# A fixed TensorE round for an attention and gated feed-forward kernel, with another start and paced loads

## The chip, the cores and the metric

The kernel runs on one core of one Trainium2 chip. The metric is the device time of one execution in microseconds (us).

## The reference, cut to what matters

```python
# q, k, v: (4 batches, 8 heads, 768 positions, 64); blocks of 32 positions
scores = q @ k.T / 8
mask   = |block_i - block_j| <= 1, or first/last block row or column, or one of 3 sampled blocks per row
attn   = softmax(where(mask, scores, -1e9)) @ v
x      = attn as (3072 tokens, 512)
out    = (sigmoid(x @ w_gate) * (x @ w_val)) @ w_out        # 512 -> 1536 -> 512, float32 out
```

## The kernel before

All matrices are float16, sums float32. Work is cut into 12 groups of 256 queries (4 batches times 3), and each group into 4 head pairs, so there are 48 head pairs. A head pair needs:

- three **score tiles** (128 keys x 2, 2 heads, 256 queries). The head dimension is 64, so a score matmul fills half of the array's rows, and the two heads run side by side. A tile takes two banks of PSUM.
- an exponential of each tile on ScalarE (ACT), and a multiplication by the mask on VectorE (DVE).
- **values**: 24 full-array matmuls, one bank.

A group of 256 queries then needs 12 **gate** steps (8 matmuls of 256 columns, one bank, a tanh on ACT, a product on DVE) and two **outputs** of 12 matmuls of 512 columns, one bank each.

The program is not written in the order in which it runs. Every operation goes into a plan with an estimated time, what it reads and writes, and a priority; a greedy list scheduler in Python fixes the order on each engine before anything is built. Each engine then runs its list strictly in order and waits where a real duration differs from the plan.

```python
SINGLE, PAIR = (7, 6, 5, 4), (0, 2)          # banks of all else; pairs of banks of the scores
...
st = psb([2, 512], homes=(0, 2, 4) if n < 1 else PAIR, span=2)      # a score tile
o  = P.op("PE", 0.43 if masked else 0.215, scores, ..., prio=seq, mode="row", behind=scored[-1:])
o.paired = not masked                         # after full-array work, wait until two tiles fit
...
if e == "PE":
    if o.mode != mode:                        # the plan's price of going from "row" to "full" or back
        dur += 0.095
```

The start: the mask tables go out on ACT's DMA queue, the identity and the first keys on SyncE's (SP), everything else on GpSimd's (POOL). TensorE (PE) is kept busy with dummy matmuls ("spins" on a tile of zeros) until data are there:

```python
P.op("SP", 0.4, lambda: nc.sync.dma_start(ident16(), id_h.ap()), writes=[ident16], prio=-99, dma=0.1)
P.op("ACT", 0.4, lambda: nc.scalar.dma_start(sbi(), sampled_blocks), writes=[sbi], prio=-90, dma=0.1)
P.op("ACT", 0.4, lambda: nc.scalar.dma_start(mi(), mi_h.ap()), writes=[mi], prio=-89, dma=0.1)
...
o = self.spin_op(0.11 if now < 12.0 else 0.06, fresh)     # a dummy matmul, where PE has nothing planned
```

The softmax here doesn't subtract the row's maximum and nothing guards it: scores larger than these inputs give would overflow.

Of the kernel before, what the change touches and what calls it, by code (L numbers as in the profile page):

```python
# [20 lines left out]
NCH = 3  # L21
# [8 lines left out]
NMASK = 1  # L30
EDGES = [0, 768, 1536]
FIRST = [
    ("q", 0), ("k", 1), ("q", 1), ("k", 2), ("q", 2), ("v", 0), ("k", 3), ("q", 3), ("v", 1), ("v", 2), ("v", 3),
# [22 lines left out]
class Op:  # L56
    def __init__(self, ways, deps, allocs, prio, mode, dma, behind):
        self.ways, self.deps, self.allocs = ways, deps, allocs
        self.prio, self.mode, self.dma, self.behind = prio, mode, dma, list(behind)
        self.eng = self.start = self.end = self.seen = None  # L60
        self.paired = False
        self.slack = 0.0
# [5 lines left out]
class Plan:  # L68
# [16 lines left out]
    def op(self, eng, dur, fn, reads=(), writes=(), after=(), prio=0, mode=None, dma=0.0, behind=(), alt=()):  # L85
        deps, allocs = list(after), []
        ways = {eng: (dur, fn), **{e: (t, f) for e, t, f in alt}}
        o = Op(ways, deps, allocs, prio, mode, dma, behind)
        for b in reads:
            deps.extend(b.writers)  # L90
            b.users.append(o)
        for b in writes:
            if not b.users and b.ring is not None:
                allocs.append(b)
                if b.ring in self.queued:
                    b.turn = self.queued[b.ring]
                    self.queued[b.ring] += 1
            else:
                deps.extend(b.users if b.ring is None else b.writers)
            b.users.append(o)  # L100
            b.writers.append(o)
        self.ops.append(o)
        return o

    def run(self):
# [23 lines left out]
        def places(allocs, eng):  # L129

            t, where, taken = 0.0, [], set()
            for b in allocs:
                if b.ring in self.queued:
                    s = slot(b.ring, 0, eng) if b.turn == at[b.ring] else None
                    where.append(at[b.ring] % len(self.rings[b.ring]))
                else:
                    can = []
                    for i in b.homes:
                        at_, old = now, self.rings["ps"][i : i + b.span]
                        for k, u in enumerate(old):  # L140
                            s = None if i + k in taken else clear(u, eng)
                            at_ = None if s is None or at_ is None else max(at_, s)
                        if at_ is not None:
                            can.append((at_, self.spun is not None and self.spun in old, len(can), i))
                    s, _, _, i = min(can) if can else (None, 0, 0, None)
                    taken.update(range(i, i + b.span) if can else ())
                    where.append(i)
                if s is None:
                    return None, None
                t = max(t, s)  # L150
            return t, where
# [11 lines left out]
        while left:  # L163
            wake = []
            for e in LAT:
# [54 lines left out]
                if o.dma:  # L220
                    first = now + (3.2 if e == "POOL" else 1.9)
                    if o.dma > 0.15:
                        first = dma_free = max(dma_free, first) + o.dma
                    o.seen = first + 0.3 + o.slack
                else:
                    o.seen = o.end + LAT[e]
# [27 lines left out]
def kernel(  # L254
# [15 lines left out]
    e24_np = np.zeros((128, NJ * 128), np.float16)  # L270
    for r in (0, 64):
        e24_np[r : r + NB] = tok.reshape(1, -1) // BLK == np.arange(NB)[:, None]
# [34 lines left out]
    SINGLE, PAIR = (7, 6, 5, 4), (0, 2)  # L307
# [16 lines left out]
    def one(shape, dt, name):  # L324
# [11 lines left out]
    P.op("SP", 0.4, lambda: nc.sync.dma_start(ident16(), id_h.ap()), writes=[ident16], prio=-99, dma=0.1)  # L336
    P.op("ACT", 0.4, lambda: nc.scalar.dma_start(sbi(), sampled_blocks), writes=[sbi], prio=-90, dma=0.1)
    P.op("ACT", 0.4, lambda: nc.scalar.dma_start(mi(), mi_h.ap()), writes=[mi], prio=-89, dma=0.1)
    P.op(
        "SP", 0.5, lambda: nc.sync.dma_start(e24().rearrange("b j q -> b (j q)"), e24_h.ap()),  # L340
        writes=[e24], prio=-94.5, dma=0.5,
    )
# [19 lines left out]

    stage, half16, tr, v16 = {}, {}, {}, {}
# [41 lines left out]
    def load_half(nm, b, p, prio, dur=0.72):  # L405
        c = sb(f"{nm}16" if nm != "v" else "vh", [128, 2, NJ, 64], f16)
        half16[nm, b, p] = stage[nm, b, p] = c
        o = P.op(
            "POOL", dur, lambda: nc.gpsimd.dma_start(c(), src[nm][b][:, 2 * p : 2 * p + 2]),  # L409
            writes=[c], prio=prio, dma=1.0,  # L410
        )
        o.slack = 0.3 + b
        return o

    def turn_pe(nm, b, p, js, prio, behind=()):

        n = js.stop - js.start
        c = half16[nm, b, p]
        if (nm, b, p) not in tr:
            tr[nm, b, p] = sb(f"{nm}T", [128, NJ, 128], f16)  # L420
        t = tr[nm, b, p]
        g = psb([n, 128], f16)

        def go():
            for j in range(n):
                for hd in range(2):
                    nc.tensor.transpose(
                        g()[hd * 64 : hd * 64 + 64, j, :], c()[:, hd, js.start + j], ident16()
                    )

        P.op("PE", 0.06 * n, go, reads=[c, ident16], writes=[g], prio=prio, mode="col", behind=behind)
        P.op(
            "DVE", 0.1 + 0.075 * n, lambda: nc.vector.tensor_copy(t()[:, js], g()), reads=[g], writes=[t],
            prio=prio,
        )
# [11 lines left out]
    every, early, later = slice(0, NJ), slice(0, 2), slice(2, NJ)  # L447
    load("k", 0, 0, -95)
    t, c = stage["k", 0, 0], one([128, 2, NJ, 64], f16, "k16_first")
    half16["k", 0, 0] = c  # L450
    P.op("ACT", 0.83, lambda t=t, c=c: nc.scalar.copy(c(), t()), reads=[t], writes=[c], prio=-67)
    for i, (nm, p) in enumerate(FIRST):
        last_in = load_half(nm, 0, p, -60 + i, 0.82 if i == 0 else 0.72)
    for p in range(NP):
        turn_pe("k", 0, p, every, -40 + 2 * p)
        turn_pe("q", 0, p, early, -39.5 + 2 * p)
        cast_v(0, p, -30 + p)
# [21 lines left out]
    def load_out(s, prio, behind):  # L479
        def go():  # L480
            ins = nc.gpsimd.dma_start(wo()[:, 4 * s : 4 * s + 4], wov[:, 4 * s : 4 * s + 4])  # L481
            if s == 2:
                landed["o"] = ins

        o = P.op(
            "POOL", 0.8, go,
            prio=prio, dma=2.65, behind=behind,
        )
        for f in range(4 * s, 4 * s + 4):
            w_out[f] = o  # L490
# [16 lines left out]
    def blocks():  # L507
# [7 lines left out]
        for r in (0, 64):  # L515
            d.tensor_tensor(mb16()[:, r : r + NB], eqs()[:, 0], eqs()[:, 1], op=ALU.max)

    P.op("DVE", 0.65, blocks, reads=[sbi, mi], writes=[mb16, eqs], prio=-70)
    for c, j0, n in ((0, 0, 2), (1, 2, 4)):
# [6 lines left out]
            reads=[mb16, e24], writes=[pb], prio=-69 + 32.5 * c, mode="full",  # L526
# [6 lines left out]
            reads=[pb], writes=[bias], prio=-69 + 32.5 * c,  # L533
        )

    mask_ops = {}
# [31 lines left out]
    def attend(n, p, seq):  # L568
# [3 lines left out]
        for tt in range(NCH):  # L572
            st, pt = psb([2, 512], homes=(0, 2, 4) if n < 1 else PAIR, span=2), sb("pt", [128, 2, 2, CH], f16)
# [19 lines left out]
            )  # L593
            scored.append(o)
            o.paired, o.twin = not masked, psb([2, 512], homes=PAIR, span=2)
# [32 lines left out]
        valued[n, p] = P.op("PE", 0.79, values, reads=[*pts, v16[b, p]], writes=[o], prio=seq + 0.1, mode="full")  # L628
# [42 lines left out]
    def ffn(g, seq):  # L671
# [4 lines left out]
        for f in range(NF):  # L676
            both = psb([512], homes=range(7, -1, -1) if last else SINGLE)
# [36 lines left out]
        for tt in range(w // 128):  # L714
# [5 lines left out]
            for u in range(parts):  # L720
                m = slice(u * wd, u * wd + wd)
                py = psb([DM], homes=range(7, -1, -1) if g >= len(GROUPS) - 2 else SINGLE)
                for f0 in range(0, NF, 4):

                    def go(f0=f0, tt=tt, py=py, m=m):
                        for f in range(f0, f0 + 4):
# [7 lines left out]
                            "PE", 0.862 / parts, go, reads=[hts[g, f] for f in range(f0 + 4)], writes=[py],  # L734
# [18 lines left out]
    seq, turned = 0, []  # L753
    for n in range(B * NCH):
        b, c = divmod(n, NCH)
        if n == 1:
            for p in range(NP):
                turn_pe("q", 0, p, later, 9.0, [valued[0, 1]])
            build_mask(1, 11.5, scored[:1])
# [5 lines left out]
        if b + 1 < B:  # L765
            for p in range(NP) if c == 0 else ():
# [5 lines left out]
                for nm in "kqv":  # L772
                    o = load(
                        nm, b + 1, p, seq + p, behind=turned[:-2][-2:],
                        **(dict(after=[w_out[8]], sync="o") if b == 0 else {}),
                    )
                    o.slack = 1.5
                for nm in "kq":
# [4 lines left out]
    for (n, p), o in valued.items():  # L783
        g = group_of[n][0] - 2
        if g >= 0:
            o.behind.append(gates[2 * NF * (g + 1) - 1])
    P.run()
# [30 lines left out]
```

## Time and profile before

297.87 us (median of 3; 297.75 to 298.46). The lines of the page that say what the kernel spends: span, busy time by engine, PE's busy tenths in 40 slices, and the granted clock of PE in tenths.

```profile
span 295.6 us, 8119 instructions
...
PE 289.7 (98%) x3417; PEld 211.3 (72%) x3417; DVE 192.4 (65%) x448; ACT 212.5 (72%) x329; POOL 13.4 (5%) x22
...
PE   8999998999999999999999999999999999999995
...
PEclk9999999999999999999999999999999999999999
```

PE is the bound. "Busy" is not the same as useful, though. The timeline of PE in the steady part shows what is lost (columns: start, duration of the group, engine, line, operation, matrices, shapes, count; in later views [idle time before, and what ended it, the "releaser"]; L582 scores, L683 gates, L727 outputs, L621 values):

```profile
190.77 0.61 PE L582 MATMUL psum<-qT,kT 64*128 64x256 f16 x8
191.32 2.76 PE L727 MATMUL psum<-wo,h 128*128 128x512 f16 x12
194.01 0.61 PE L582 MATMUL psum<-qT,kT 64*128 64x256 f16 x8
194.56 0.61 PE L683 MATMUL psum<-x,wg 128*128 128x256 f16 x4
195.00 0.60 PE L683 MATMUL psum<-x,wv 128*128 128x256 f16 x4
```

Take starts, not ends, since matmuls overlap. Gates to gates is 0.44 us for four matmuls. Two score tiles are four side-by-side pairs of 0.109 us, which is 0.436, but the next group starts 0.55 us after them (194.01 to 194.56); and the outputs need 12 x 0.2158 = 2.59 us, but 2.69 pass until the next scores. So each batch of score tiles costs about 0.10 us going in and 0.11 coming out, 0.21 us in all. PE never stands idle there for any releaser; the time goes at the change of the array's layout. The Trainium skill ("TensorEngine Tiling (Array Packing)", section "Key Properties") says that a change of tiling mode drains TensorE, that is, lets the work in it run out; it names no cost. The trace fits that: the first gate's weight load starts at 194.55, with its matmul, where later ones start 0.1 us ahead of theirs.

In the trace of before there are 77 batches of scores, 49 of them from the 17th head pair on (46 of two tiles, 3 of one). The count ahead of the 17th, 28, leaves out short pieces between mask steps and looks past transposes and dummies; with every uninterrupted run of score matmuls counted it is 42.

### The profile page before, as it was taken

What the parts mean: (1) busy time and instruction counts of PE and PEld (TensorE: products, weight loads), DVE (VectorE), ACT (ScalarE), POOL (GpSimd) and SP (SyncE); (2) the same over time, 40 slices, a digit from 0 to 9 for tenths busy, and PEclk for the clock granted to TensorE, in tenths of its full rate; (3) what the DMA queues carried; (4) which work ended last, traced back from release to release, by engine and by line L of the source; (5) the groups of instructions that cost most, each with busy time, mean ns of one, the idle gap of its engine ahead of it and who ended that gap; (6) DMA issues with size and microseconds to landing.
All of it is one profiled execution on the core that took longest, in us unless ns stands there. A gap on an engine that the chain in (4) does not pass through costs nothing.

```text
span 295.6 us, 8119 instructions
## 1 busy us (share of the span) xinstructions
PE 289.7 (98%) x3417; PEld 211.3 (72%) x3417; DVE 192.4 (65%) x448; ACT 212.5 (72%) x329; POOL 13.4 (5%) x22
## 2 busy tenths in 40 slices
PE   8999998999999999999999999999999999999995
PEld 7676875786587587578578678667767768778673
DVE  3659995799677677577767657657657656634230
ACT  2699987889888789797588578478478478434331
POOL 8630000000000000000000000000000000000000
PEclk9999999999999999999999999999999999999999
DMA  7999969999999969940210210210120120120102
GB/s 157 199 211 210 206 171 283 311 297 271 272 244 248 228 96 308 172 115 2 62 47 0 65 47 3 55 54 2 31 77 2 27 83 3 27 82 0 38 35 72
DMA packets 50316, 35.56 MB, mean 120 GB/s; under 512 B 31080, under 2 KB 47336, under 8 KB 50280
## 3 DMA queue, kind: packets, MB, share of 16 engines
q1 hardware_dynamic: 43520, 28.16, 38.5%
q0 software_dynamic: 6688, 6.88, 14.1%
q8 instruction: 26, 0.43, 0.6%
q14 instruction: 10, 0.08, 0.1%
q10 hardware_dynamic: 72, 0.01, 0.0%
HBM read 28.55 MB, written 6.29 MB: 118 GB/s over the span
## 4 chain that ended last, share of the span: by engine, by line
PE 82%; DMA 13%; POOL 2%; issue 1%; SPq 0%; ACT 0%; DVE 0%; POOLq 0%
PE psum L683 40%; PE psum L727 21%; PE psum L582 10%; PE psum L621 10%; DMA wo<-in_moe_w_out_dram 8%; DMA q<-in_q_dram 3%; DMA vs<-in_v_dram 2%; POOL q L409 1%; POOL k L409 1%; POOL wo L481 1%; SPq L371 0%; POOL vh L409 0%; PE psum L657 0%; DVE h L709 0%; ACT tg L702 0%
## 5 line engine op out<-in xcount | busy, mean ns | idle before, releaser
L598 ACT ACTIVATE pt<-psum 128x1024 f16<-128x1024 f32 x144 | 143.9, 1025 | 38.1 <-PE psum L582 37.9
L606 DVE TENSOR_TENSOR pt<-pt,mask 128x1024 f16<-128x1024 f16 x132 | 90.4, 689 | 44.1 <-ACT pt L598 43.7
L683 PE MATMUL psum<-x,wg 128*128 128x256 f16 x576 | 86.6, 273 | 0.2 <-DVE h L709 0.2
L683 PE MATMUL psum<-x,wv 128*128 128x256 f16 x576 | 86.7, 273 | 0.0
L709 DVE SCALAR_TENSOR_TENSOR h<-tg,psum 128x256 f16<-128x256 f32 x144 | 56.8, 416 | 21.3 <-ACT tg L702 21.2
L727 PE MATMUL psum<-wo,h 128*128 128x512 f16 (+1 forms) x300 | 66.8, 371 | 0.0
L702 ACT ACTIVATE tg<-psum 128x256 f32<-128x256 f32 x144 | 55.2, 388 | 14.1 <-PE psum L683 11.3
L683 PEld LDWEIGHTS <-wg 128*128 128x128 f16 x576 | 54.7, 98 | 11.5 <-issue 4.2
L683 PEld LDWEIGHTS <-wv 128*128 128x128 f16 x576 | 53.8, 98 | 11.9 <-issue 6.1
L727 PEld LDWEIGHTS <-h 128*128 128x128 f16 x300 | 27.5, 98 | 30.6 <-issue 4.0
L582 PE MATMUL psum<-qT,kT 64*128 64x256 f16 x576 | 48.5, 272 | 0.3 <-ACT pt L598 0.3
L621 PEld LDWEIGHTS <-pt 128*128 128x128 f16 x1152 | 40.4, 97 | 4.3 <-issue 1.3
L621 PE MATMUL psum<-v,pt 128*128 128x65 f16 x1152 | 42.2, 193 | 0.0
L582 PEld LDWEIGHTS <-kT 64*128 64x128 f16 x576 | 23.4, 94 | 14.5 <-issue 11.0
L744 ACT ACTIVATE y<-psum 128x512 f32<-128x512 f32 (+1 forms) x21 | 12.1, 577 | 21.9 <-PE psum L727 20.0
L632 DVE TENSOR_TENSOR x<-psum,rz 128x256 f16<-128x256 f32 x48 | 20.4, 424 | 1.6
L629 DVE RECIPROCAL rz<-psum 128x4 f32<-128x4 f32 x48 | 8.6, 179 | 15.6 <-PE psum L621 15.1
L356 PE MATMUL psum<-zero 128*128 128x128 f16 x49 | 5.7, 296 | 1.0 <-DVE zero L335 1.0
L582 PE MATMUL psum<-bias,e 64*128 64x256 f16 x48 | 6.3, 273 | 0.0
L402 ACT CAST q<-qs 128x768 f16<-128x768 f32 x6 | 5.0, 833 | 1.8 <-DMA qs<-in_q_dram 1.8
L552 DVE TENSOR_SCALAR mask<-psum 128x512 f16<-128x512 f32 x9 | 6.1, 683 | 0.0
L356 PEld LDWEIGHTS <-zero 128*128 128x128 f16 x49 | 4.7, 138 | 1.8 <-DVE zero L335 1.0
(43 smaller groups left out, 72.4 us busy)
## 6 DMA issues: line engine op xcount, KB each, us to landing
out_dram<-y SPq DMA_DIRECT2D x23, 256.0 KB, 2.4
ks<-in_k_dram SPq DMA_DIRECT2D x13, 384.0 KB, 4.1
qs<-in_q_dram SPq DMA_DIRECT2D x12, 384.0 KB, 5.4
vs<-in_v_dram SPq DMA_DIRECT2D x12, 384.0 KB, 5.0
wg<-in_moe_w_gate_dram POOLq DMA_DIRECT2D x2, 768.0 KB, 14.2
wv<-in_moe_w_val_dram POOLq DMA_DIRECT2D x2, 768.0 KB, 17.0
wo<-in_moe_w_out_dram POOLq DMA_DIRECT2D x3, 512.0 KB, 21.8
q<-in_q_dram POOLq DMA_DIRECT2D x4, 192.0 KB, 6.2
```

Source lines behind the costliest of these rows:

```text
L356: "PE", dur, lambda: nc.tensor.matmul(t(), zero(), zero(), start=True, stop=True),
L582: nc.tensor.matmul(st()[:, hd, jj * CH : (jj + 1) * CH], l[r, 2 * tt + jj, :], m[r, 2 * c : 2 * c + 2, :], start=not (own and masked), sto ...
L598: lambda st=st, pt=pt: nc.scalar.activation(pt().rearrange("p h j q -> p h (j q)"), st(), AF.Exp, scale=SCALE),
L606: nc.vector.tensor_tensor(t, t, mask()[:, c, tt].unsqueeze(1).to_broadcast([128, 2, 512]), op=ALU.mult)
L621: nc.tensor.matmul(o()[:, 2 * jq + hd, 0:65], pts[j // 2]()[:, hd, j % 2, jq * 128 : jq * 128 + 128], v_[:, hd, j, 0:65], start=(j == 0), ...
L629: P.op("DVE", 0.2, lambda: nc.vector.reciprocal(rz(), o()[:, :, 64:65]), reads=[o], writes=[rz], prio=seq - 5)
L632: lambda: nc.vector.tensor_tensor(x16().rearrange("p j (h d) -> p (j h) d", d=64), o()[:, :, 0:64], rz().to_broadcast([128, 4, 64]), op=AL ...
L683: nc.tensor.matmul(t()[:, z : z + w], wt()[:, i, f * 128 : (f + 1) * 128], xT[g, i]()[:, 0:w], start=(i == 0), stop=(i == NP - 1),)
L702: lambda tg=tg, a=pair[0]: nc.scalar.activation(tg()[:, 0:w], a[0]()[:, a[1] : a[1] + w], AF.Tanh, scale=0.5),
L709: lambda tg=tg, a=pair[1], h_=h_: nc.vector.scalar_tensor_tensor(h_()[:, 0:w], tg()[:, 0:w], 1.0, a[0]()[:, a[1] : a[1] + w], op0=ALU.add, ...
L727: nc.tensor.matmul(py()[:, m], hts[g, f]()[:, tt * 128 : (tt + 1) * 128], wo()[:, f, m], start=(f == 0), stop=(f == NF - 1),)
L744: lambda py=py, y=y, m=m: nc.scalar.activation(y()[:, m], py()[:, m], AF.Copy, scale=0.5),
```

## The change

Its intent: from the 17th head pair on, PE repeats one round for each head pair: three score tiles together (six of the eight banks), one output slice, the values of the head pair before, three gate steps, two output slices. Banks are no longer parted: all work may use all eight. The loads of a later batch wait for a given round. And the start is rebuilt, to bring the first score earlier. The core of the diff (cut):

```diff
+FETCH = ((7, 1), (1, 2))
+CHAIN, GLAG, OLAG, ROUND = 16, 5, 9, "SoVgggoo"
+LAND_K, LAND_Q, E24 = 4.0, 4.7, 4.2        # when the plan takes the first loads to be there
-    SINGLE, PAIR = (7, 6, 5, 4), (0, 2)
+    SINGLE, PAIR = range(7, -1, -1), (0, 2, 4, 6)
-    P.op("SP", 0.4, lambda: nc.sync.dma_start(ident16(), id_h.ap()), writes=[ident16], prio=-99, dma=0.1)
-    P.op("ACT", 0.4, lambda: nc.scalar.dma_start(sbi(), sampled_blocks), writes=[sbi], prio=-90, dma=0.1)
-    P.op("ACT", 0.4, lambda: nc.scalar.dma_start(mi(), mi_h.ap()), writes=[mi], prio=-89, dma=0.1)
+    P.op("ACT", 0.4, lambda: nc.scalar.dma_start(ident16(), id_h.ap()), writes=[ident16], prio=-99, dma=0.1, lands=3.0)
+    P.op("ACT", 0.6, lambda: nc.scalar.dma_start(sbi(), sampled_blocks), writes=[sbi], prio=-98, dma=0.1, lands=3.4)
+    P.op("ACT", 0.4, lambda: nc.scalar.dma_start(mi(), mi_h.ap()), writes=[mi], prio=-97, dma=0.1, lands=3.8)
...  (the first keys in one float32 load, cast in two parts; a third of the first queries in a load of its own;
...   the mask for the first 256 queries built first, the rest later; output steps of two matmuls, not four)
-            o.paired, o.twin = not masked, psb([2, 512], homes=PAIR, span=2)
+            o.paired, o.twin = not masked and 4 * n + p < CHAIN, psb([2, 512], homes=PAIR, span=2)
+    chain, gi, oi = [], 6 * (CHAIN - GLAG), 3 * max(0, CHAIN - OLAG)
+    for m in range(CHAIN, len(score) + 8):
+        for step in ROUND:
+            if step == "S":
+                chain += score[m] if m < len(score) else []
+            elif step == "V":
+                chain += value[m - 1 : m]
+            elif step == "g":
+                chain += gates[gi : gi + 2]
+                gi += 2
+            elif m >= OLAG:
+                chain += outs[oi : oi + 1]
+                oi += 1
+    chain += outs[oi:]
+    for a, z in zip(chain, chain[1:]):
+        z.behind.append(a)                    # in the plan, each only after the one ahead of it
+    for m, o in late_loads:
+        o.behind.append(score[m][-1])         # loads paced by round
```

## The prediction

> **What bounds the kernel now.** TensorE. The page gives PE 289.7 us busy of 295.6 (98%), ACT 72%, DVE 65%; the clock is 1.0 throughout. The view of waits puts only about 3 us on PE; the chain of waits is 82% PE. Busy is not work, so I added start-to-start intervals of the trace: a gate matmul of 256 columns 109.2 ns, an output matmul of 512 columns 215.8, a value matmul 31.8, a pair of half-array score matmuls 109. (The Trainium skill, "TensorE: Matmul & The Clock Gate", section "Back-to-back issue gap", gives N/2.4 + 2.5 ns; the trace agrees.) From the first score (8.38 us) to the last matmul (292 us) there are 283.6 us, of which 262.9 are such work. Of the other 20.7 about 15 are switches between half-array scores and full-array work: the timeline shows 0.095 us lost going in and as much coming out, 0.19 us for a batch of scores, and there are 77 batches. Real waits after 8.4 us are about 2.5 us (0.9 of it at 48 us).
>
> **What the change does.**
> 1. Fixed round from the 17th head pair on: three score tiles together. The 96 tiles there now go in 49 or 50 batches; after, 32. That saves 17 to 18 switches of 0.19 us: 3.4 us, all on the critical path, as PE never waits there. The matmul work is unchanged: a round is 0.65 + 0.19 scores, 1.30 output, 0.76 values, 2.62 gates: 5.5 us.
> 2. Will the round stall? It costs ACT 3 exponentials (0.97), 3 tanh (0.38), half an eviction (0.3): 4.3 us; DVE 3 masks (0.65), 3 products (0.42), 0.6: 3.8 us. Six banks for scores leave two, for an output in progress and the last gate; that gate's bank comes free about 0.3 us into the round, a finished output's at about 1.0 us, before values at 1.28. Narrow but enough; I allow 0.8 us of new waits.
> 3. The start: the first head pair's keys and half its queries come by themselves, cast in parts. The first score should start near 6.2 us (estimate: landing, plus 0.35 cast, 0.3 transposes, 0.3 copy). But up to 25 us PE has only scores and values, and ACT (9 tenths busy there, 1.0 us a tile) feeds those, so not all is kept: 1.5 us.
> 4. Loads paced by round, all eight banks for all: no work saved; the wait at 48 us may go: 0.4 us. The tail (3.2 us after the last matmul) stays.
>
> Sum: -3.4 - 1.5 - 0.4 + 0.8 = -4.5 to -5: **predicted 293.0 us, 8 in 10 between 289.8 and 295.8**. Faster by over 2% (under 291.9): 0.33; within 2%: 0.65; slower by over 2%: 0.02.
>
> **What would show it.** Score batches from the 17th head pair: 32, of 12 matmuls each; from that pair's first score to the last matmul 3 to 4 us shorter. PE waits inside rounds under 1 us in total; round period near 5.5 us. First score near 6.2 us, but the first gate hardly earlier than 25.35. ACT and DVE busy times equal within 3 us.
>
> **What would make it wrong.** Real exponentials and masks take longer than the plan's (0.915, 0.61 us), so a round could wait for banks; 0.2 us in each of 32 rounds takes all back. Transposes of attention outputs share the DMA queue with paced loads; a late one stalls gates that can no longer be reordered. Or the weights land earlier and PE gains more at the start: under 291 us.

## The result, and the profile after

294.38 us (median of 4; 293.13 to 295.25), before 297.81 (median of 4). The ratio is 0.988, with a 95% interval of 0.984 to 0.992. (Here and below a ratio is the mean time of one kernel's fast runs over that of the other's in the same rounds, so it is not quite the ratio of the medians.) The page after:

```profile
span 292.5 us, 8112 instructions
...
PE 285.4 (98%) x3411; PEld 212.2 (73%) x3411; DVE 193.4 (66%) x451; ACT 210.2 (72%) x329; POOL 13.4 (5%) x22
...
PE   5999999999999999999999999999999999999995
...
PEclk9799999999999999999999999999999999999999
```

Two digits have changed for the worse, at the very start: PE's first slice and the clock's second one. The rest is PE at 9. One round in the steady part (L617 scores, L764 outputs, L658 values, L720 gates):

```profile
191.75 0.83 PE L617 MATMUL psum<-qT,kT 64*128 64x256 f16 x12
192.51 0.61 PE L764 MATMUL psum<-wo,h 128*128 128x512 f16 x2
192.95 0.93 PE L658 MATMUL psum<-v,pt 128*128 128x65 f16 x24
193.71 0.60 PE L720 MATMUL psum<-x,wg 128*128 128x256 f16 x4
...
196.33 1.03 PE L764 MATMUL psum<-wo,h 128*128 128x512 f16 x4
197.29 0.83 PE L617 MATMUL psum<-qT,kT 64*128 64x256 f16 x12
```

Every round from the 18th head pair on takes 5.54 or 5.55 us from score to score, to the last scores; no round waits. There are 33 batches of scores from the 17th head pair on, 31 of them of 12 matmuls (three tiles), where before had 49. In front of the 17th there are 19, where before had 28 (31 and 42 with every uninterrupted run counted).

Now the start. The timeline after, cut to what the first score waits for (ACTq and SPq lines are DMA issues):

```profile
0.73 0.41 ACTq L342 DMA_DIRECT2D ident<-bb_ident  x1
...
1.91 0.30 ACTq L344 DMA_DIRECT2D mi<-bb_mdet_iota  x1
...
6.74 0.22 DVE L540 TENSOR_TENSOR eqs<-mi,sbi 24x72 f32<-24x72 f32 x1 [5.08 <-DMA mi<-bb_mdet_iota]
...
7.55 0.28 PE L557 MATMUL psum<-e,mb 24*128 24x256 f16 x1 [2.36 <-DVE mb L546]
7.69 0.41 ACT L475 CAST q_a<-q_in 128x256 f16<-128x256 f32 x1 [2.69 <-DMA q_in<-in_q_dram]
...
8.91 0.85 PE L441 MATMUL psum<-ident,k 128*64 128x128 f16 x12
9.16 0.37 ACT L449 COPY qT<-psum 128x256 f16<-128x256 f16 x1 [0.69 <-PE psum L441]
...
10.48 0.40 PE L617 MATMUL psum<-bias,e 64*128 64x256 f16 x2
...
10.66 0.42 PE L617 MATMUL psum<-qT,kT 64*128 64x256 f16 x2
...
10.88 0.42 PE L617 MATMUL psum<-bias,e 64*128 64x256 f16 x2
```

The same places before:

```profile
1.38 0.31 ACTq L338 DMA_DIRECT2D mi<-bb_mdet_iota  x1
...
3.78 0.22 DVE L509 TENSOR_TENSOR eqs<-mi,sbi 24x72 f32<-24x72 f32 x1 [2.52 <-DMA mi<-bb_mdet_iota]
...
8.38 0.28 PE L582 MATMUL psum<-bias,e 64*128 64x256 f16 x2
...
8.50 0.27 PE L582 MATMUL psum<-qT,kT 64*128 64x256 f16 x2
...
8.61 0.27 PE L582 MATMUL psum<-bias,e 64*128 64x256 f16 x2
```

A table `mi` of 4.5 KB landed at 6.7 us instead of 3.8, although it was issued only 0.5 us later. In the trace's DMA records its data packets ran between 4.4 and 6.1 us, after the identity (1.8 to 3.2) and the sampled blocks (3.3 to 4.2) on the same queue and between packets of the key load and of POOL's loads; the engines were 90% busy or more from 2.7 us on. Before, they ran between 2.6 and 3.3 us, though the engines were as busy from 2.7 us on there too. The Trainium skill ("DMA: Bandwidth & Descriptors", section "Queues, rings and completion order") says that each DMA engine goes round the queues packet by packet; these records agree with that. The query slice landed 5.9 us after its issue, at 7.7, where the plan had 4.7. And the first score stood about 1 us more behind the transposes of the second head pair (from 8.91), which the plan had put ahead of it: its own queries were in place at 9.53.

So the first score came at 10.48 us, 2.1 us later than before, not 2.2 us earlier. This is one execution. Four of the experiments below keep these first instructions as they are, but for a dummy, and their profiles have the table in use at 5.6 (no_pace), 5.7 (four_banks), 5.8 (no_round) and 6.9 us (split_scores), and the first score at 8.3, 8.4, 9.7 and 10.8 us. So the start of the changed kernel varies by more than 2 us from one execution to the next, and a first score that comes 1 us earlier in one profile doesn't show by itself what an edit did. And the score pairs started 0.21 us apart, not 0.11 (10.66 to 10.88 against 8.50 to 8.61): PE ran at half clock. The trace's clock records have full clock from 4.92 to 8.34 us, half to 11.75, then full; in the window before, PE had stood idle for 2.4 us, since the planned dummies ran out at 5.2. The skill ("TensorE: Matmul & The Clock Gate", "What's actually happening") describes this: a window of 3413 ns whose activity sets the clock, full or half. Here too the change came in steps of 3.41 us.

To add up the two profiled executions, I took from elapsed time what PE's work needs at full rate (0.1092 us for a gate matmul, 0.2158 for an output of 512 columns, 0.0318 for values, 0.1092 for a score pair, 0.03 and 0.06 for transposes, dummies nothing). What is left is lost time, in us:

| stretch | before | after | difference |
|---|---|---|---|
| to the first score (8.38 / 10.48 us) | 7.1 | 9.3 | +2.2 |
| from there to the 17th head pair (78.9 / 82.9 us) | 10.2 | 8.5 | -1.7 |
| from there to the last matmul (292.1 / 289.2 us) | 10.5 | 7.1 | -3.4 |

The sum, -2.9 us, is the difference of the last matmuls' starts (292.11 and 289.17).

Of the -1.7 us in the second row, waits that went away make up most. Before, PE waited 1.4 us there, the longest time at 49 us for an attention output that it had to transpose (from the view of waits):

```profile
PE psum L657 <- DVE x L632: 0.7, 1, 0.7
```

After, it waited 0.1 us in the whole stretch. Against that, half clock until 11.75 us cost after about 0.6 us (half of 1.27).

### The profile page after: what moved, and what is told of

It is laid out like the page before. It is cut to its first block, busy times and chain, and to the rows that moved or that the text cites. A ratio compares the mean times of both kernels' runs of the same rounds, so it can differ in the third digit from the quotient of the medians.

```text
span 292.5 us, 8112 instructions
## 1 busy us (share of the span) xinstructions
PE 285.4 (98%) x3411; PEld 212.2 (73%) x3411; DVE 193.4 (66%) x451; ACT 210.2 (72%) x329; POOL 13.4 (5%) x22
## 4 chain that ended last, share of the span: by engine, by line
PE 91%; ACT 4%; DMA 2%; DVE 1%; issue 1%; ACTq 0%; DVEq 0%
PE psum L720 43%; PE psum L764 22%; PE psum L617 12%; PE psum L658 12%; ACT pt L635 3%; DMA mi<-bb_mdet_iota 2%; PE psum L441 1%; PE psum L579 1%; DVE pt L643 1%; PE psum L694 0%; PE psum L364 0%; ACT y L781 0%; ACTq L343 0%; PE psum L557 0%; DVE k L409 0%
## 5 line engine op out<-in xcount | busy, mean ns | idle before, releaser
L635 ACT ACTIVATE pt<-psum 128x1024 f16<-128x1024 f32 x144 | 139.0, 1031 | 21.4 <-PE psum L617 21.1
L720 PE MATMUL psum<-x,wv 128*128 128x256 f16 x576 | 86.5, 273 | 0.0
L720 PE MATMUL psum<-x,wg 128*128 128x256 f16 x576 | 86.4, 272 | 0.0
L764 PE MATMUL psum<-wo,h 128*128 128x512 f16 (+1 forms) x300 | 76.0, 372 | 0.1
L720 PEld LDWEIGHTS <-wv 128*128 128x128 f16 x576 | 55.7, 98 | 7.6 <-issue 1.3
L720 PEld LDWEIGHTS <-wg 128*128 128x128 f16 x576 | 53.3, 98 | 8.3 <-issue 1.5
L658 PEld LDWEIGHTS <-pt 128*128 128x128 f16 x1152 | 42.6, 98 | 9.6 <-issue 0.6
L617 PE MATMUL psum<-qT,kT 64*128 64x256 f16 x576 | 45.2, 272 | 0.0
L658 PE MATMUL psum<-v,pt 128*128 128x65 f16 x1152 | 44.3, 193 | 0.0
L764 PEld LDWEIGHTS <-h 128*128 128x128 f16 x300 | 25.9, 98 | 22.4 <-issue 8.0
L617 PEld LDWEIGHTS <-kT 64*128 64x128 f16 x576 | 25.1, 94 | 19.1 <-issue 16.1
L781 ACT ACTIVATE y<-psum 128x512 f32<-128x512 f32 (+1 forms) x23 | 13.3, 580 | 12.7 <-PE psum L764 12.7
L617 PE MATMUL psum<-bias,e 64*128 64x256 f16 x48 | 6.3, 289 | 0.0
L402 ACT CAST v<-vs 128x768 f16<-128x768 f32 x7 | 5.9, 842 | 0.0
L409 DVE CAST q<-qs 128x768 f16<-128x768 f32 x10 | 5.5, 553 | 0.5 <-DMA qs<-in_q_dram 0.5
```

The costliest lines, as they stand in the source:

```text
L617: nc.tensor.matmul(st()[:, hd, jj * CH : (jj + 1) * CH], l[r, 2 * tt + jj, :], m[r, 2 * c : 2 * c + 2, :], start=not (own and masked), sto ...
L635: lambda st=st, pt=pt: nc.scalar.activation(pt().rearrange("p h j q -> p h (j q)"), st(), AF.Exp, scale=SCALE),
L658: nc.tensor.matmul(o()[:, 2 * jq + hd, 0:65], pts[j // 2]()[:, hd, j % 2, jq * 128 : jq * 128 + 128], v_[:, hd, j, 0:65], start=(j == 0), ...
L720: nc.tensor.matmul(t()[:, z : z + w], wt()[:, i, f * 128 : (f + 1) * 128], xT[g, i]()[:, 0:w], start=(i == 0), stop=(i == NP - 1),)
L764: nc.tensor.matmul(py()[:, m], hts[g, f]()[:, tt * 128 : (tt + 1) * 128], wo()[:, f, m], start=(f == 0), stop=(f == NF - 1),)
L781: lambda py=py, y=y, m=m: nc.scalar.activation(y()[:, m], py()[:, m], AF.Copy, scale=0.5),
```

## The experiments

Theory A: the round gains by saving switches of the array's layout; the new start loses about 2 us. Rival B: the start is hidden behind ACT and the loads and worth nothing either way, so that the whole gain is the 17 switches that the prediction counted. Theory D was added later: the start's loss is partly PE's clock.

The numbers of all runs, each beside the runs of before on the same chip:

| run | median (lowest to highest) us | ratio to before | 95% interval |
|---|---|---|---|
| after | 294.38 (293.13 to 295.25) | 0.988 | 0.984 to 0.992 |
| round_old_start | 292.85 (291.75 to 294.66) | 0.984 | 0.979 to 0.989 |
| start_old_round | 299.62 (299.27 to 300.34) | 1.006 | 1.004 to 1.009 |
| mask_first | 293.41 (292.5 to 294.13) | 0.984 | 0.981 to 0.988 |
| split_scores | 307.67 (306.66 to 308.64) | 1.033 | 1.029 to 1.037 |
| start_fixed | 295.26 (294.38 to 296.2) | 0.993 | 0.989 to 0.997 |
| no_round | 297.03 (295.97 to 297.8) | 0.999 | 0.995 to 1.002 |
| no_pace | 298.2 (297.05 to 300.2) | 1.003 | 0.998 to 1.009 |
| four_banks | 331.82 (one run) | | |
| more_spins | 293.31 (292.17 to 293.48) | 0.985 | 0.982 to 0.987 |
| mask_first_spins | 293.44 (292.71 to 293.98) | 0.986 | 0.984 to 0.988 |
| best | 292.53 (291.79 to 292.83) | 0.983 | 0.980 to 0.985 |
| eight_banks | 299.43 (298.54 to 300.46) | 1.006 | 1.003 to 1.008 |

All gave correct results. In the sections below, "late" batches are those from the 17th head pair on.

### The two halves of the change alone

round_old_start is the changed kernel with the first 8 us of before:

```diff
 # on the changed kernel: back to before's identity, tables and mask building
-    P.op("ACT", 0.4, lambda: nc.scalar.dma_start(ident16(), id_h.ap()), ..., lands=3.0)
+    P.op("SP", 0.4, lambda: nc.sync.dma_start(ident16(), id_h.ap()), ..., dma=0.1)
...
-    P.op("SP", 0.5, lambda: nc.sync.dma_start(k_in(), src["k"][0][:, 0:2]), ...)     # and q_in, their casts
+    load("k", 0, 0, -95)
...
```

> The changed kernel with the first 8 us of the kernel before (its loads, queues, casts and mask building), all else as changed. Theory A (the round and the free bank order save about 25 switches of 0.19 us, 4.8 us; the new start loses about 2 us because the first score comes at 10.5 instead of 8.4 us): first score near 8.4 us, 292.0 to 292.8 us. Rival B (the start is hidden behind ScalarE and the weights and is worth nothing either way; the whole 3.4 us is the 17 switches): 294.2 to 294.6 us.

start_old_round is the kernel before with just those lines of the new start.

> The kernel before with only the new start. Theory A: first score near 10.5 us and 299.3 to 300.3 us, slower than before by about 2 us. Rival B: 297.6 to 298.0 us.

The new start alone made the old kernel slower by 0.6%, its interval clear of 1. The time is as A expected, and it is against B. The way there is not quite A's: in the profile the first score came at 9.54 us, not 10.5, and 0.6 us of the loss is a longer wait at 52.6 us (1.36 us, where before waited 0.74 at 49 us), since the scheduler makes the whole plan anew when the start changes. The round with the old start gave 292.85, just above what A expected (292.0 to 292.8); its interval overlaps that of the changed kernel, so time alone doesn't show that it is faster. Its runs fell apart: 291.75, 292.08, 293.61 and 294.66 (of which 290.0, 290.3, 290.7 and 292.9 lie between the first instruction and the last). The last is the profiled one; in it PE stood idle for 1.0 us ahead of the first query transposes (not at all in the profile of before), had half clock from 7.2 to 14.0 us, and the first score came at 9.1 us.

### What the mask tables' place in the queue is worth

```diff
 # on the changed kernel: the tables ahead of the identity on ACT's queue
-    ... writes=[ident16], prio=-99, dma=0.1, lands=3.0)
-    ... writes=[sbi], prio=-98, dma=0.1, lands=3.4)
-    ... writes=[mi], prio=-97, dma=0.1, lands=3.8)
+    ... writes=[ident16], prio=-96.5, dma=0.1, lands=3.8)         # a higher number goes later
+    ... writes=[sbi], prio=-98, dma=0.1, lands=3.0)
+    ... writes=[mi], prio=-97, dma=0.1, lands=3.4)
```

> The changed kernel with the two small mask tables ahead of the identity matrix on their DMA queue. Theory A (TensorE sat idle 2.4 us for the table that landed at 6.7 us behind 32 KB of identity, then ran at half clock): the table lands before 4.5 us, no wait of over 1 us on it, first score near 9.5 us (then the query slice, which landed at 7.7 us, is last), 292.5 to 293.6 us. Rival B: 294.2 to 294.6 us. Rival C (the table is late because all 16 DMA engines are full, whatever its place in the queue): it still lands after 6 us and nothing changes.

The timeline of this run, at the same places as before:

```profile
1.41 0.30 ACTq L344 DMA_DIRECT2D mi<-bb_mdet_iota  x1
...
4.72 0.22 DVE L540 TENSOR_TENSOR eqs<-mi,sbi 24x72 f32<-24x72 f32 x1 [3.06 <-DMA mi<-bb_mdet_iota]
...
9.35 0.40 PE L617 MATMUL psum<-bias,e 64*128 64x256 f16 x2
```

The table landed 2.0 us earlier (0.8 us or more before that of any execution with the old order) and the first score came 1.1 us earlier, with the query slice now last (7.0 us); the median fell by 1.0 us, though the intervals overlap. The rival that its place in the queue does not matter is out. The clock was no better here: half until 12.9 us in the profiled run, and that took the 1.1 us back (half of the 2.25 us for which the scores ran longer at half clock): the last matmul started at 289.0 us, against 289.2. So the traces don't show where the 1.0 us of the medians came from.

### What a switch costs

```diff
 # on the changed kernel
-CHAIN, GLAG, OLAG, ROUND = 16, 5, 9, "SoVgggoo"
+CHAIN, GLAG, OLAG, ROUND = 16, 5, 9, "sosVsgggoo"        # s: one score tile
```

> The changed kernel with the three score tiles of a round apart, each between full-array work: 96 batches for the same 96 tiles instead of 32 or 33. If a switch into and out of half-array scores costs 0.19 us, 63 more cost 12 us: 306 to 307 us, round period 5.92 us instead of 5.545. If instead the gain came from the order of the other work or from the banks, the time stays within 2 us of 294.4.

The timeline of PE in one round of this run:

```profile
200.41 0.39 PE L617 MATMUL psum<-qT,kT 64*128 64x256 f16 x4
200.74 0.60 PE L764 MATMUL psum<-wo,h 128*128 128x512 f16 x2
201.28 0.39 PE L617 MATMUL psum<-qT,kT 64*128 64x256 f16 x4
201.60 0.94 PE L658 MATMUL psum<-v,pt 128*128 128x65 f16 x24
```

95 late batches instead of 33, and 13.3 us more in the medians: 0.21 us for each. The round's period is 5.97 us instead of 5.545, which is the same 0.21 us twice. The order of the other work is as it was and no round waits, so the number of batches is what counts. Expected were 306 to 307 us; most of the excess is the switch being 0.21 rather than 0.19 (62 times 0.02 is 1.2 us).

### The round without its parts

no_round leaves the plan free to the end, with all else of the change:

```diff
-CHAIN, GLAG, OLAG, ROUND = 16, 5, 9, "SoVgggoo"
+CHAIN, GLAG, OLAG, ROUND = 99, 5, 9, "SoVgggoo"
```

> The changed kernel without its fixed round (the plan orders TensorE freely to the end), all else kept. If the round's gain is the 16 to 17 switches it saves from the 17th head pair on: 49 or more batches there, 297.3 to 298.0 us. If the eight banks for all alone gave the gain: within 0.7 us of 294.4.

297.03 us, a little under the range, and no longer different from before. With four pairs of banks to choose from the free plan makes 45 late batches, fewer than the 49 I had expected. The lost time from the 17th head pair on is 10.2 us against 7.1 with the round; the 12 batches explain 2.3 to 2.5 of the 3.1.

four_banks keeps the round but parts the banks as before:

```diff
-    SINGLE, PAIR = range(7, -1, -1), (0, 2, 4, 6)
+    SINGLE, PAIR = (7, 6, 5, 4), (0, 2)
```

> The changed kernel with the banks parted as before: scores in two pairs of banks, all else in the other four. The third score tile of a round must then wait for the first one's exponential (about 1.0 us and 0.4 us of latencies, against 0.22 us for the second tile): round period 6.5 to 6.9 us instead of 5.545, 325 to 335 us in all. If six banks are not what makes the round work: within 2 us of 294.4.

```profile
200.41 0.61 PE L617 MATMUL psum<-qT,kT 64*128 64x256 f16 x8
202.08 0.39 PE L617 MATMUL psum<-qT,kT 64*128 64x256 f16 x4 [1.06 <-ACT pt L635]
```

The third tile stands 1.06 us before the first one's exponential has freed its banks; the round's period is 6.6 to 6.8 us, and the kernel takes 331.82 us. So three tiles together need six banks, and six banks need the freed partition.

eight_banks is the other way about: before, with only the freed banks.

```diff
 # on the kernel before, with the new way to choose a bank
-    SINGLE, PAIR = (7, 6, 5, 4), (0, 2)
+    SINGLE, PAIR = range(7, -1, -1), (0, 2, 4, 6)
...
-            st, pt = psb([2, 512], homes=(0, 2, 4) if n < 1 else PAIR, span=2), ...
+            st, pt = psb([2, 512], homes=PAIR, span=2), ...
```

> The kernel before with only the freed banks (any work in any of the eight banks, scores in any of four pairs); no round, no new start, no pacing. The plan then makes 66 batches of scores instead of 77. If fewer batches are what the banks give: 11 times 0.19 us, 295.4 to 296.2 us, useful work and waits unchanged, and fewer batches ahead of the 17th head pair too (the 1.7 us there that the prediction had not foreseen). If the banks alone give nothing and the gain there came from elsewhere: 297.3 to 298 us.

This was a clear miss. The trace has some 61 batches, 16 fewer than before (41 of them late, by any way of counting), and yet the kernel is 0.6% slower. Lost time was 10.9 us from the first score to the 17th head pair (before 10.2) and 11.7 after it (before 10.5). The waits of PE in this run:

```profile
...
PE psum L659 <- DVE x L634: 0.7, 1, 0.7
PE psum L546 <- ACT pt L600: 0.5, 1, 0.5
PE psum L584 <- ACT pt L600: 0.5, 1, 0.5
```

Scores and mask steps (L584, L546) wait for exponentials to give banks back, and there are repeated stops of 0.2 us at gates after 180 us, each ending just as a product on DVE ends. So where all work shares the banks, a free order saves switches and pays for them with waits. Only the round, which was laid out so that nothing waits for a bank, keeps the saving. That the small stops are bank waits follows from their timing alone; the view names no releaser for them.

### Pacing of the loads

```diff
 # on the changed kernel
-    for m, o in late_loads:
-        o.behind.append(score[m][-1])
```

> The changed kernel with loads of later batches not paced by the round. If pacing saves no work and only avoids waits of the attention transposes behind loads: 0 to 1 us slower, waits of TensorE on transposed inputs after 90 us if anything; theory: 294.2 to 295 us.

A second miss, and a larger one: 298.2 us, all of the gain gone. From the waits of PE:

```profile
PE psum L720 <- DMA x<-x: 2.2, 1, 2.2
...
PE psum L720 <- DVE x L669: 0.8, 1, 0.8
```

From 94.1 to 96.2 us the gates wait 2.2 us for the transpose of an attention output, which goes over the same DMA queue as the unpaced loads; this is one of the risks that the prediction had named. In a fixed round nothing else may go ahead. This idle time also cost clock: the records have half clock from 97.2 to 100.7 us. From the 17th head pair on (84.1 us here) the lost time is 13.1 us, against 7.1 in the changed kernel; the two waits above and the half clock make up 4.7 of these 6 us (3.0 waited, and half of 3.4); four shorter waits at 84 to 86 and at 130 us, 1.5 us together, are about the rest. The first score came at 8.3 us here, so the loss would have been larger with the start of the changed kernel's profile.

### The start repaired by order of loads

```diff
 # on mask_first: query slice and keys ahead of the mask pattern on SP's queue,
 # landing times as traces showed them, the first head pair's scores planned first
-LAND_K, LAND_Q, E24 = 4.0, 4.7, 4.2
+LAND_K, LAND_Q, E24 = 4.7, 3.4, 5.0
...
-                writes=[st], prio=seq, mode="row", behind=scored[-1:],
+                writes=[st], prio=seq if n or p else -50, mode="row", behind=scored[-1:],
...
-        o.slack = 0.3 + b
+        o.slack = 1.8
```

> The changed kernel with the mask tables first on their queue, the query slice and the keys first on the other, landing times in the plan set to what the traces showed, and the first head pair's scores planned ahead of the second pair's transposes. Theory A (each us by which the first score comes earlier is worth about 1 us until some 7 us, because TensorE is the bound from there on): first score at 6.6 to 7.6 us, 290.0 to 292.0 us. Rival B (before 25 us ScalarE and the weights bound it, so a start earlier than that of the kernel before, 8.4 us, is worth nothing more): 292 to 293 us, with TensorE waiting between 10 and 27 us.

It failed, and does not decide between A and B. The table and the query slice were there by 3.5 us, but now the identity, last on its queue, came at 6.7:

```profile
6.73 0.30 PE L441 MATMUL psum<-ident,q_a 128*64 128x128 f16 x4 [1.70 <-DMA ident<-bb_ident]
```

The first score came at 8.49 us, at half clock until 11.3 us; and the plan, which follows from every number in it, brought new waits: 1.5 us of PE between 73 and 89 us. The small transfer issued last was late in both: the table after, the identity here.

### The clock

```diff
 # on the changed kernel: more dummy matmuls in the same idle stretches of the plan
-                        o = self.spin_op(0.11 if now < 12.0 else 0.06, fresh)
+                        o = self.spin_op(0.06 if now < 12.0 else 0.06, fresh)
```

> The changed kernel with 29 more dummy matmuls in the first idle stretch (64 instead of 35) and 5 more by the first score, nothing else. Theory D (TensorE's idle time before 8 us puts its clock to half at 8 to 12 us, just when real work begins, and that, with the late first score, is what the new start loses): no half clock after 8.5 us, transposes and first scores at full rate, 292.2 to 293.6 us, and the runs closer together than the 2.1 us of the changed kernel. Rival: half clock there costs nothing since the stretch to 25 us is bound by ScalarE and loads: 294 to 294.8 us.

The timeline of PE in this run:

```profile
1.40 6.18 PE L364 MATMUL psum<-zero 128*128 128x128 f16 x64 [1.40 <-DVE zero L340]
7.50 0.28 PE L557 MATMUL psum<-e,mb 24*128 24x256 f16 x1
...
9.58 0.28 PE L617 MATMUL psum<-bias,e 64*128 64x256 f16 x2
9.70 0.27 PE L617 MATMUL psum<-qT,kT 64*128 64x256 f16 x2
9.80 0.27 PE L617 MATMUL psum<-bias,e 64*128 64x256 f16 x2
```

The mask work starts when it did (7.50 against 7.55): the table was late again (in use at 6.3 us), and the longer row of dummies held PE 0.4 us beyond the mask that was made from it (ready at 7.1). But full clock holds from 6.5 us on, the pairs start 0.11 us apart, and the first score comes 0.9 us earlier. The last matmul starts at 288.4 us instead of 289.2. The median is 293.31, 1.1 us under the changed kernel (0.9 by the ratios) and in the range of D; the runs span 1.3 us instead of 2.1. The two ratios' intervals overlap between 0.984 and 0.987, so the time alone would not prove it. What the trace shows is full clock at the first scores, in the one execution that was profiled; an earlier first score is within what the start varies by, and no_pace had full clock there (until 97 us) without more dummies.

mask_first_spins adds the tables' order of mask_first:

> The same dummy matmuls with the mask tables first on their queue. Theory D: first score near 8.8 us at full clock, 291.4 to 292.6 us. Rival: as the run with the mask tables first alone, 293.0 to 293.8 us.

293.44: no better than the dummies alone, and a miss for D. The reason that its trace shows: 59 dummies, most of them at half clock, held PE until 7.5 us, so that the mask work started no earlier than in more_spins though the mask was ready at 5.5. Dummies that outlast the wait become the wait.

### A version that beats both

best takes the round, banks and pacing of the changed kernel, the loads of before, and the mask of the first 256 queries built first, then:

```diff
-                writes=[st], prio=seq, mode="row", behind=scored[-1:],
+                writes=[st], prio=seq if n or p else -38.75, mode="row", behind=scored[-1:],
...
-                        o = self.spin_op(0.11 if now < 12.0 else 0.06, fresh)
+                        o = self.spin_op(0.08 if now < 12.0 else 0.06, fresh)
```

> A try at a version better than both: round, banks and pacing of the changed kernel, the loads of the kernel before, mask building for the first query chunk alone, first scores planned before the second pair's transposes, dummy matmuls planned at 0.08 us. First score near 7.8 to 8.2 us at full clock: 290.3 to 291.8 us. If what the plan does later (waits at 60 to 100 us, as in an earlier attempt) eats it: 292 to 294 us.

The timeline of PE at its first scores (L593):

```profile
8.47 0.28 PE L593 MATMUL psum<-bias,e 64*128 64x256 f16 x2
8.59 0.27 PE L593 MATMUL psum<-qT,kT 64*128 64x256 f16 x2
```

First score at 8.47 us, full clock from 6.2 us on, as many batches as the changed kernel but one, no wait of over 0.25 us after the first score, the last matmul at 286.9 us. It took 292.53 us, 1.7% under before and the lowest median of all. Expected were 290.3 to 291.8: the first score came 0.3 to 0.7 us later than hoped for, and the rest I cannot place. Against the changed kernel it is better in the median by 1.9 us (1.5 by the ratios), but the two ratios come from different rounds on other chips, and their intervals overlap slightly (0.984 to 0.985).

## Why the prediction was right or wrong

294.38 us lies in the range (289.8 to 295.8), in the likelier class (within 2%), and 1.4 us above the number given. The sum was near, and partly by luck: of its terms one had the wrong sign, and other errors made up for about half of that. Against the table above the start was wrong by 3.7 us (a loss of 2.2 where a gain of 1.5 was forecast), while the stretch up to the 17th head pair gained 1.3 us more than the 0.4 forecast and the 0.8 us of new waits did not come: together 1.6 us too optimistic, -2.9 measured for -4.5.

- **Bound by PE, and the cost of a switch:** right. Lost time, not busy time, was the right thing to count, though a switch costs 0.21 us (from the starts above, from the round's period and from splitting the batches), not 0.19.
- **Step 1, the round saves 17 to 18 switches, 3.4 us:** right. 33 late batches instead of 49, lost time there 3.4 us less: 16 batches at 0.21 us, where the prediction had 17 to 18 at 0.19. Without the round the gain is gone.
- **Step 2, 0.8 us of new waits:** too much. The rounds waited for nothing, and the period was 5.545 us. With the banks parted a round waits 0.9 to 1.06 us, so the banks do matter; how much margin six leave was not measured.
- **Step 3, "the first score should start near 6.2 us", worth 1.5 us:** this step failed. The estimate took the plan's landing times as if they were facts. The table and the query slice landed at 6.7 and 7.7 us, transposes of the second pair stood ahead of the first score, it came at 10.48, and idle PE brought half clock besides. In the profiled executions the start cost 2.2 us where it was to bring 1.5; the size varies (first score at 8.3 to 10.8 us with the same instructions), and the direction rests on the new start in the old kernel, 1.8 us slower over four runs. The argument that PE is fed by ACT up to 25 us, so that only part of the start counts, got no support: after the first score PE waited 0.1 us at most up to the 17th head pair, and in the profiles the last matmul moved with the first score and the clock together (0.8 us earlier for a first score 0.9 us earlier with more dummies; 0.1 us earlier for one 1.1 us earlier with the tables first, where half clock lasted 1.1 us longer). The clause "First gate hardly earlier than 25.35" held in the weak sense that it came later, at 26.86.
- **Step 4, paced loads and free banks, 0.4 us:** mis-sized. In front of the 17th head pair 1.7 us were gained. The wait at 48 us did go (0.74 us), and with it 0.6 us of shorter ones; as half clock took about 0.6 us back, about 1 us is left for the fewer batches there (19 instead of 28), an estimate from these sums. Which part of the change brings fewer batches without waits is open: free banks alone make about as few there but pay in waits. And pacing is not a matter of 0.4 us: in the new kernel its loss costs 3.8 us between the medians (4.6 by the ratios).
- **Tail:** unchanged, 3.5 us from the last matmul's start before, 3.3 after.

## What to carry to other kernels

Where PE is full, count start-to-start intervals against the work's own rate: here that showed 0.2 us for each batch of half-array work, which no wait and no busy share showed, and it said beforehand what a fixed round is worth. A fixed order keeps such a gain only if everything that it waits for (banks, transposes, loads) is laid out around it, and without that a freer order loses less. At the start of a kernel do not trust planned landing times: small transfers issued behind or among large ones came 2 to 3 us later than planned, by amounts that changed from one execution to the next, and in the changed kernel's profile idle PE time there was paid twice, the second time by the clock. Look at more than one execution of a start before you trust its size.

## What the Trainium skill lacked or had wrong

- "TensorEngine Tiling (Array Packing)", "Key Properties": says that a mode switch drains TensorE, but not what that costs. Here about 0.10 us going into half-array work and 0.11 coming out; 0.21 us for each further batch when batches were split.
- "TensorE: Matmul & The Clock Gate", "Why this matters for your kernels", advises no idle gaps over about 3 us. Here 2.4 us idle in a 3.41 us window (1.0 us covered by matmuls) brought half clock for the next one; in another run a window with 2.1 us covered did so, and in a third one with 2.3 us covered did not.
- "DMA: Bandwidth & Descriptors" tells how queues are served; I found no figure there for what a small transfer waits among large ones. Here a 4.5 KB table took 2.4 us from issue to use when issued at 1.4 us (3.3 in mask_first, 2.0 in start_fixed), and 3.7 to 5.0 us in six executions when issued at 1.9 us behind 32 KB on its queue.
- "TensorE: Matmul & The Clock Gate", "Back-to-back issue gap": gives N/2.4 + 2.5 ns for a matmul of N columns as the gap of isolated matmuls, and about 131 ns for 512 columns in a real stream of weight loads and matmuls. Here the first figure held in such a stream: 109.2 ns for 256 columns, 215.8 for 512.
